# k and v of batch 2 in the row layout of q, and two vector-engine operations moved, in a fused linear-attention and SwiGLU kernel

## The chip, the cores and the metric

The kernel runs on one core of a Trainium2 chip. The metric is the device time of one execution in microseconds. Before the change the median was 326.07 us over three runs (326.01 to 326.35).

The engines are called by short names: PE is the matmul engine, PEld its weight loads, ACT the scalar engine, DVE the vector engine, POOL the GpSimd engine, SP the engine whose queue issues most of the DMAs.

## The reference

The program computes linear attention for 8 batches of 8 heads, 576 tokens and 64 columns, and puts its result through a gated feed-forward layer (512 to 1536 to 512).

```python
def phi(x, c, s):                       # c, s: cos and sin of pi/2 * pos/576
    r = np.maximum(x, 0.0)
    return np.concatenate([r * c, r * s], axis=-1)
q_p, k_p = phi(q, cos_w, sin_w), phi(k, cos_w, sin_w)
kv  = np.einsum('bhsf,bhsd->bhfd', k_p, v)      # sum over the 576 tokens
z   = np.sum(k_p, axis=2)
num = np.einsum('bhsf,bhfd->bhsd', q_p, kv)
den = np.einsum('bhsf,bhf->bhs', q_p, z)[..., None] + 1e-06
x   = (num / den).transpose(0, 2, 1, 3).reshape(4608, 512)
# ---- feed-forward
xn  = x / np.sqrt(np.mean(x * x, -1, keepdims=True) + 1e-06) * rms_g
g   = xn @ w_gate
out = (g / (1 + np.exp(-g))) * (xn @ w_val) @ w_out
```

## The kernel before

The feed-forward layer runs in nine blocks of 512 tokens: blocks 0 to 7 are the first 512 tokens of each batch, block 8 gathers the last 64 tokens of all eight. A block has 12 steps (two products of 4 wide matmuls, a Silu on ACT, a product on DVE) and 4 output steps. The attention of the next batch is hung between those steps: `at(block, step, place, function, ...)` puts a call there.

There are two layouts for k and v. The **dense** layout treats the 8 heads of a batch as one long run, 4 pairs of heads each spread over 128 partitions; a partition holds 9 tokens of one head, and one head fills 64 partitions:

```python
def load_kv(which, b, r0=0, r1=4, j0=0, j1=NJ):      # NJ = 9; one DMA
    ... in_=src[b, 2*r0:2*r1].rearrange("h s d -> (h s d)")
             .rearrange("(r p n) -> p r n", p=P, n=NJ * D)
def k_phi(eng, b, j, part, rs=(0, 4)):               # one scaling per token slot j: 9 of 256 columns
    ...
def kvz_mm(b, banks, rs=(0, 4)):
    for r in range(*rs):
        for j in range(NJ):
            for c in range(2):
                lo = 64 * c                          # 64 rows: half of the array
                nc.tensor.matmul(banks[c][:, r*E:(r+1)*E],
                    lhsT=kp_main[b][lo:lo+64, j, r, :], rhs=vvm[b % 2][lo:lo+64, r, j, :],
                    start=(j == 0), stop=(j == NJ - 1))      # 4 * 9 * 2 = 72 matmuls
```

The layout **of q** gives every head all 128 partitions with 4 tokens each, and treats the last 64 tokens of each head apart, in a tail:

```python
def load_heads(which, b, h0, h1):                    # tokens 0..511 of some heads, rows of 4 tokens
    ...
def load_last(which, b):                             # tokens 512..575: two DMAs of 64 KB
    ...
def k_phi_as_q(eng, b, c, part):                     # 4 scalings of 512 columns, one of 256
    ...
def v_cast_as_q(eng, b, h0, h1):                     # two casts on DVE
    ...
def v_cast_last(eng, b):                             # two small casts of the tail, on POOL
    ...
def kvz_as_q(b, pst):
    for h in range(H):
        for c in range(5):                           # 8 * 5 = 40 matmuls of 128 rows
            nc.tensor.matmul(pst[:, h % 2, h//2*E:(h//2+1)*E], lhsT=kp_of(b)[...],
                rhs=vv_of(b)[:, c, h, :] if c < 4 else vvt[b % 2][:, h, :], ...)
```

Batches 0 to 2 are dense in the kernel before, batches 3 to 7 have the layout of q. The turn from the outputs of block 0 to block 1 reads as follows (`tr1(j, ...)` is a PE transpose of x and an ACT copy `xnT<-psV`; `x_sq` squares and sums on ACT, with a small power on POOL; `x_norm` and `out_store(V, ...)` run on DVE):

```python
    for n in range(NNT - 2):
        ...
        if n in nd_at:                       # n = 4, 6, 8, 9
            ...
            x_sq(1, j)
        ...
    x_norm(1, 2)
    tr1(1, psV[1][:, :])
    for j in (2, 3):
        for n in (NNT - 2, NNT - 1):
            out_mm(0, j, n, banks0[j])
    out_store(V, 0, 2, banks0[2])
    out_store(A, 0, 3, banks0[3])
    for j in (0, 1):
        for n in (NNT - 2, NNT - 1):
            out_mm(0, j, n, banks0[j])
    gval_mm(1, 0, 0, (0, 256))               # first matmuls of block 1
    ...
```

The program ends with the last output tile in two halves, each copied by ACT and stored by two DMAs, one from SP and one from ACT.

Of the kernel before, what the change touches and what calls it, by code (L numbers as in the profile page):

```python
# [26 lines left out]
def kernel(  # L27
# [30 lines left out]
    psA = ps.tile([P, 2, 512], FP32, name="psA")  # L58
# [8 lines left out]
    V, A, G = nc.vector, nc.scalar, nc.gpsimd  # L67
    NJ = 9
    LOW, HIGH = (0, 2), (2, 4)
# [4 lines left out]
    def load_kv(which, b, r0=0, r1=4, j0=0, j1=NJ):  # L74

        key = (which, b)
        if key not in raw:
            raw[key] = (two if which == "k" else one).tile(
                [P, 4, NJ * D], FP32, name=f"r{which}", tag=f"r{which}"
            )  # L80
        src = {"k": k, "v": v}[which]
        return nc.sync.dma_start(
            out=raw[key][:, r0:r1, j0 * D : j1 * D],
            in_=src[b, 2 * r0 : 2 * r1, :, :]
            .rearrange("h s d -> (h s d)")
            .rearrange("(r p n) -> p r n", p=P, n=NJ * D)[:, :, j0 * D : j1 * D],
        )
# [31 lines left out]
    def load_heads(which, b, h0, h1):  # L119
        src = {"k": k, "v": v}[which]  # L120
        nc.sync.dma_start(
            out=kv_tile(which, b)[:, h0 * 4 * D : h1 * 4 * D].rearrange(
                "p (h n) -> p h n", n=4 * D
            ),
            in_=src[b, h0:h1, 0:512, :].rearrange("h (p j) d -> p h (j d)", j=4),
        )
# [131 lines left out]
    def k_phi(eng, b, j, part, rs=(0, 4)):  # L258

        o = slice(0, D) if part == 0 else slice(D, F)  # L260
        f = cos_of if part == 0 else sin_of
        if b not in kp_main:
            kp_main[b] = one.tile([P, NJ, 4, F], BF16, name="kpm", tag="kpm")
        phi(
            eng, kp_main[b][:, j, rs[0] : rs[1], o],
            raw[("k", b)][:, rs[0] : rs[1], j * D : (j + 1) * D], f(5 + j),
        )
# [237 lines left out]
    def x_norm(b, j):  # L505
        xn = four.tile([P, DM], BF16, name="xn", tag="xn")
        nc.vector.scalar_tensor_tensor(  # L507
            out=xn[:, :], in0=x_of[(b, j)][:, 0:DM], scalar=rs_of[(b, j)][:, :], in1=gb[:, :],
            op0=ALU.mult, op1=ALU.mult,
        )  # L510
        xn_of[(b, j)] = xn
# [22 lines left out]
    def x_tr_evac(eng, b, j, bank, part=(0, 4)):  # L534
        dst = bank.bitcast(BF16).rearrange("p (t s) -> p t s", s=P)
        copy(eng, x_dst(b, j)[:, part[0] : part[1], :], dst[:, part[0] : part[1], :])
# [5 lines left out]
    def gval_mm(blk, n, bank, cols=(0, TB), parts=((psG, wg), (psV, wv))):  # L542
        x = xnT[blk]
        for pst, w in parts:
            for t in range(NDT):
                nc.tensor.matmul(  # L546
                    pst[bank][:, cols[0] : cols[1]],
                    lhsT=w[:, t, n * P : (n + 1) * P],
                    rhs=x[:, t, cols[0] : cols[1]],
                    start=(t == 0), stop=(t == NDT - 1),  # L550
                )
# [19 lines left out]
    def out_store(eng, blk, j, bank):  # L571
        osb = four.tile([P, DM], FP32, name="osb", tag="osb")
        copy(eng, osb[:, :], bank)
        rows0 = out[0:S, :].rearrange("(p j) m -> j p m", j=NJ)
        if blk == 0:
            for i in range(2):
                nc.sync.dma_start(
                    out=rows0[2 * j + i, :, :], in_=osb[64 * i : 64 * i + 64, :]
                )
        elif blk < 8:  # L580
            rows = out[blk * S : blk * S + 512, :].rearrange("(p j) m -> p j m", j=4)
            nc.sync.dma_start(out=rows[:, j, :], in_=osb[:, :])
        else:
            for i in range(2):
                r0 = (2 * j + i) * S + 512
                nc.sync.dma_start(
                    out=rows0[8, :, :] if i + j == 0 else out[r0 : r0 + 64, :],
                    in_=osb[64 * i : 64 * i + 64, :],
                )
# [181 lines left out]
    def at(blk, n, where, f, *args):  # L771
        slots.setdefault((blk, n), none())[where].append((f, args))
# [26 lines left out]
    for nb in range(2, B):  # L799
        b = nb - 1  # L800
        late = nb == 2
        vb, vn = (b, 3) if late else (b - 1, 14)
        if nb == 3:
            vb, vn = b, 1
        if late:
            at(vb, vn, "post", v_cast, V, nb, *LOW)
            for j in range(NJ):
                if j > 3:
                    at(b, 1 + j // 7, "post", k_phi, V, nb, j, 0)
                if j > 1:  # L810
                    at(b, 1 + j // 7, "post", k_phi, A, nb, j, 1)
        else:
            for c in range(5):
                at(b - 1, 12 + (c * 3) // 5, "post", k_phi_as_q, V, nb, c, 0)
                at(b - 1, 12 + (c * 3) // 5, "post", k_phi_as_q, A, nb, c, 1)
        for c in range(5):
            qn = (2, 3, 5, 5, 6)[c] if late else c
            at(b, qn, "post", q_phi, V, nb, c, 0)
            at(b, qn, "post", q_phi, A, nb, c, 1)
            at(b, qn, "post", q_tr_dma, nb, c)  # L820
        if late:
            at(vb, vn + 1, "post", v_cast, V, nb, *HIGH)
        else:
            at(vb, vn, "post", v_cast_as_q, V, nb, 0, 4)
            at(vb, vn + 1, "post", v_cast_as_q, V, nb, 4, 8)
            at(vb, vn, "post", v_cast_last, G, nb)
        kz, nds = (6, (7, 9, 11, 12)) if late else (4, (5, 7, 9, 11))
        at(b, kz, "pe", kvz_pe if late else kvz_as_q, nb, psA)
        at(b, kz, "pre", kvz_evac, A, nb, psA, 0)
        at(b, kz, "pre", kvz_evac, A, nb, psA, 1)  # L830
        for j in range(4):
            n = nds[j]
            at(b, n, "mid" if n == NNT else "pe", nd_pe, nb, j, psA)
            at(b, n, "pre", nd_post, nb, j, psA)
            at(b, n, "post", x_sq, nb, j)
            where = "pre" if n + 1 >= NNT else "post"
            at(b, n + 1, where, x_norm, nb, j)
            at(b, n + 1, where, x_tr_dma, nb, j)
        if nb % 2 == 1:
            at(b, 13, "pe", nd_pe, nb, 4, psA)  # L840
            at(b, 13, "pre", nd_post, nb, 4, psA)
            at(b, 13, "post", x_sq, nb, 4)
            at(b, 14, "post", x_norm, nb, 4)
            at(b, 14, "post", x_tr_dma, nb, 4)
    for nb in range(3, B):

        b = nb - 2
# [42 lines left out]
    for n in range(NNT - 2):  # L890
        if n == 3:
            kvz_pe(1, psA)
            kvz_evac(A, 1, psA, 0)
            kvz_evac(V, 1, psA, 1)
        if 1 <= n <= 4:
            c = n - 1
            q_tr_pe(1, c, qbank[c])
            q_tr_evac(V if c < 2 else A, 1, c, qbank[c])
        if n == 0:
            for c in (1, 2, 3):  # L900
                q_phi(V, 1, c, 0)
                q_phi(A, 1, c, 1)
        if n == 1:
            v_cast(A, 1, *LOW)
            v_cast(V, 1, *HIGH)
        if n == 3:
            d = load_q_tail(1)
            tc.add_manual_dep(d.ins, wo_dmas[1].ins.name, SYNC_DEP, reason="after wo")
            load_kv("k", 2)
            load_q(2)  # L910
            load_q_tail(2)
            load_kv("v", 2)
        if n == 7:
            x_norm(1, 0)
        if n == 9:
            x_norm(1, 1)
            tr1(0, psV[0][:, :])
        for j in range(2) if n == 9 else ():
            out_mm(0, j, n, banks0[j])
        if n in nd_at:  # L920
            j = nd_at[n]
            nd_pe(1, j, psA)
            nd_post(1, j, psA)
            x_sq(1, j)
        for j in range(2 if n == 9 else 0, 4):
            out_mm(0, j, n, banks0[j])
    x_norm(1, 2)
    tr1(1, psV[1][:, :])
    for j in (2, 3):
        for n in (NNT - 2, NNT - 1):  # L930
            out_mm(0, j, n, banks0[j])
    out_store(V, 0, 2, banks0[2])
    out_store(A, 0, 3, banks0[3])
    for j in (0, 1):
        for n in (NNT - 2, NNT - 1):
# [2 lines left out]
    out_store(A, 0, 1, banks0[1])  # L938
    tr1(2, psA[:, 0, :])
    x_norm(1, 3)  # L940
    out_store(V, 0, 0, banks0[0])
    gval_mm(1, 1, 1, (0, 256), ((psG, wg),))
    x_tr_pe(1, 3, psC[1][:, :])
    x_tr_evac(V, 1, 3, psC[1][:, :])
    gval_mm(1, 1, 1, (0, 256), ((psV, wv),))
    for j in range(4):
        k_phi(V, 2, j, 0)
    for j in range(2):
        k_phi(A, 2, j, 1)
    for n in range(2):  # L950
        gval_mm(1, n, n, (256, 512))
        gval_h(1, n, n, gval_act(1, n, n))
# [64 lines left out]
```

## Time and profile before

| | before |
|---|---|
| device time, median | 326.07 us |
| profiled execution (a run of its own), device time and span | 325.86 and 324.1 us |
| PE, DVE, ACT, POOL busy | 98, 57, 54, 12% |
| chain that ends last | 90% PE, 5% DVE, 2% ACT |
| kv product of batch 2, wide group before it to second wide group after it | 65.52 to 68.87 |
| idle of PE at the turn to block 1 | 54.90 to 55.21 |

A busy time is how long an engine has instructions in it; PE's matmuls overlap, so the printed length of a group is longer than what it costs, and one reads start to start. A group of four wide matmuls costs 0.863 us that way. With PE at 98%, a saving elsewhere counts only where PE waits.

### The profile page before, as it was taken

How to read it: one execution, taken by the hardware profiler on the slowest of the kernel's cores; microseconds unless marked ns; L12 is line 12 of the kernel's file. 1: busy time of each engine (PE TensorE's matmuls, PEld its weight loads, DVE VectorE, ACT ScalarE, POOL GpSimd, SP SyncE). 2: the span in 40 equal slices, each digit the busy share in tenths (PEclk: the TensorE clock that was granted, in tenths of full speed). 3: DMA queues.
4: the chain of work that ended last, by engine and by line, in shares of the span. 5: the costliest groups of instructions: out<-in, count | busy, mean ns of one | idle time of the engine just before them, and what ended most of it. 6: DMA issues, size and time to landing. Idle time of an engine off the chain costs nothing.

```text
span 324.1 us, 6166 instructions
## 1 busy us (share of the span) xinstructions
PE 317.8 (98%) x2284; PEld 162.2 (50%) x2284; DVE 184.7 (57%) x398; ACT 173.9 (54%) x351; POOL 39.1 (12%) x85
## 2 busy tenths in 40 slices
PE   8999999999999999999999999999999999999995
PEld 2587465555445444544454445444544444444443
DVE  6975768777666765577257745772577133203410
ACT  6974865964665466545555466455644333223321
POOL 4660202001110120012001120120011000000000
PEclk9999999999999999999999999999999999999999
DMA  7999999798899676977598769766611400020014
GB/s 272 286 200 253 307 238 345 197 172 203 164 244 265 182 208 160 240 152 203 162 215 201 156 219 211 191 163 216 127 38 33 131 32 0 27 105 0 1 32 100
DMA packets 89377, 53.90 MB, mean 166 GB/s; under 512 B 56321, under 2 KB 81921, under 8 KB 89346
## 3 DMA queue, kind: packets, MB, share of 16 engines
q1 hardware_dynamic: 82304, 48.65, 58.1%
q0 software_dynamic: 6880, 4.72, 9.9%
q8 instruction: 18, 0.29, 0.4%
q10 hardware_dynamic: 162, 0.13, 0.2%
q14 instruction: 13, 0.11, 0.1%
HBM read 37.75 MB, written 9.44 MB: 146 GB/s over the span
## 4 chain that ended last, share of the span: by engine, by line
PE 90%; DVE 5%; ACT 2%; DMA 1%; issue 1%; DVEq 0%; ACTq 0%
PE psG L546 26%; PE psC L566 26%; PE psV L546 26%; PE psA L414 2%; PE psA L370 2%; DVE kpm L254 1%; PE psG L693 1%; PE psV L693 1%; DMA rk<-in_k_dram 1%; PE psO L693 1%; PE psG L566 1%; DVE vvm L339 1%; ACT kpm L252 1%; DVE qp L254 1%; PE psA L386 1%
## 5 line engine op out<-in xcount | busy, mean ns | idle before, releaser
L561 DVE TENSOR_TENSOR hT<-psV,sg 128x512 bf16<-128x512 f32 x102 | 70.3, 689 | 95.9 <-PE psV L546 85.5
L555 ACT ACTIVATE sg<-psG 128x512 f32<-128x512 f32 x102 | 60.7, 595 | 64.8 <-PE psG L546 64.7
L546 PE MATMUL psG<-xnT,wg 128*128 128x512 bf16 (+1 forms) x368 | 92.8, 374 | 0.3 <-DVE xnT L339 0.2
L546 PE MATMUL psV<-xnT,wv 128*128 128x512 bf16 (+1 forms) x368 | 92.7, 374 | 0.0
L566 PE MATMUL psC<-wo,hT 128*128 128x512 bf16 x396 | 89.4, 379 | 0.0
L546 PEld LDWEIGHTS <-wv 128*128 128x128 bf16 x416 | 40.7, 98 | 47.3
L566 PEld LDWEIGHTS <-hT 128*128 128x128 bf16 x420 | 40.1, 98 | 46.5
L546 PEld LDWEIGHTS <-wg 128*128 128x128 bf16 x416 | 38.5, 98 | 41.2 <-DVE osb L339 0.6
L485 POOL TENSOR_TENSOR rs<-ms,mhalf 128x1 f32<-128x1 f32 x36 | 19.8, 551 | 188.7 <-ACT scr L480 188.7
L337 ACT COPY osb<-psC 128x512 f32<-128x512 f32 (+1 forms) x33 | 19.1, 579 | 43.1 <-PE psC L566 42.3
L507 DVE SCALAR_TENSOR_TENSOR xn<-xt,rs,gb 128x512 bf16<-128x512 f32 x35 | 26.5, 758 | 16.6 <-POOL rs L485 16.5
L480 ACT ACTIVATE scr<-xt 128x513 bf16<-128x513 f32 x36 | 22.8, 635 | 23.9 <-DVE xt L469 23.8
L252 ACT ACTIVATE kpm<-rk,tab 128x256 bf16<-128x256 f32 (+2 forms) x58 | 28.2, 545 | 1.5 <-DMA rk<-in_k_dram 1.5
L469 DVE TENSOR_TENSOR xt<-psA,rec 128x512 f32<-128x512 f32 x35 | 24.2, 691 | 1.2
L252 ACT ACTIVATE qp<-rq,tab 128x512 bf16<-128x512 f32 (+1 forms) x37 | 23.7, 662 | 0.0
L254 DVE TENSOR_SCALAR kpm<-rk,tab 128x128 bf16<-128x128 f32 (+2 forms) x64 | 20.3, 375 | 2.1 <-DMA rk<-in_k_dram 2.1
L254 DVE TENSOR_SCALAR qp<-rq,tab 128x512 bf16<-128x512 f32 (+1 forms) x37 | 16.1, 454 | 0.0
L414 PEld LDWEIGHTS <-qpT 128*128 128x128 bf16 x248 | 11.6, 98 | 6.8 <-ACT qpT L337 0.2
L414 PE MATMUL psA<-kvzs,qpT 128*128 128x65 bf16 x248 | 12.8, 194 | 0.1
L546 PE MATMUL psG<-xnt_tail,wg 128*128 128x512 bf16 x48 | 12.3, 379 | 0.0
L546 PE MATMUL psV<-xnt_tail,wv 128*128 128x512 bf16 x48 | 12.3, 379 | 0.0
L339 DVE CAST vvm<-rv 128x1024 bf16<-128x1024 f32 (+4 forms) x16 | 10.7, 694 | 0.0
(99 smaller groups left out, 183.0 us busy)
## 6 DMA issues: line engine op xcount, KB each, us to landing
out_dram<-osb SPq DMA_DIRECT2D x28, 256.0 KB, 2.5
rk<-in_k_dram SPq DMA_DIRECT2D x20, 256.0 KB, 3.3
rq<-in_q_dram SPq DMA_DIRECT2D x20, 256.0 KB, 3.1
rv<-in_v_dram SPq DMA_DIRECT2D x16, 256.0 KB, 3.2
rq<-in_q_dram SPq DMA_DIRECT2D x2, 1024.0 KB, 8.7
out_dram<-osb SPq DMA_DIRECT2D x14, 128.0 KB, 3.2
rv<-in_v_dram SPq DMA_DIRECT2D x3, 576.0 KB, 7.9
wo<-in_moe_w_out_dram POOLq DMA_DIRECT2D x4, 384.0 KB, 7.2
```

What stands on the lines that cost most here:

```text
L252: nc.scalar.activation(out=out_ap, in_=in_ap, func=AF.Relu, scale=scale)
L254: eng.tensor_scalar(out=out_ap, in0=in_ap, scalar1=scale, scalar2=0.0, op0=ALU.mult, op1=ALU.max)
L337: nc.scalar.copy(out=o, in_=i)
L414: nc.tensor.matmul(o[:, g, i, :], lhsT=qpT[(b, 0)][:, h, j * P : (j + 1) * P], rhs=kvz_of(b, h), start=True, stop=True,)
L469: nc.vector.tensor_tensor(out=xt[:, 0:DM].rearrange("p (b h d) -> p b h d", b=2, d=D), in0=o[:, :, :, 0:D], in1=rec[:, :, :].unsqueeze(3). ...
L480: nc.scalar.activation(out=scr[:, :], in_=xt[:, 0 : DM + 1], func=AF.Square, scale=1.0 / math.sqrt(DM), accum_out=ms[:, :],)
L485: nc.gpsimd.tensor_tensor(out=rs[:, :], in0=ms[:, :], in1=mhalf[:, :], op=ALU.pow)
L507: nc.vector.scalar_tensor_tensor(out=xn[:, :], in0=x_of[(b, j)][:, 0:DM], scalar=rs_of[(b, j)][:, :], in1=gb[:, :], op0=ALU.mult, op1=ALU. ...
L546: nc.tensor.matmul(pst[bank][:, cols[0] : cols[1]], lhsT=w[:, t, n * P : (n + 1) * P], rhs=x[:, t, cols[0] : cols[1]], start=(t == 0), sto ...
L555: nc.scalar.activation(out=sg[:, :], in_=psG[bank][:, :], func=AF.Silu)
L561: nc.vector.tensor_tensor(out=hTs[blk][:, n, :], in0=psV[bank][:, :], in1=sg[:, :], op=ALU.mult)
L566: nc.tensor.matmul(bank, lhsT=hTs[blk][:, n, j * P : (j + 1) * P], rhs=wo[:, n, :], start=(n == 0), stop=(n == NNT - 1),)
```

## The change

The intent: PE does the kv product of batch 2 with 40 matmuls on all rows instead of 72 on half of them, ACT and DVE have fewer and larger scalings, and two orders on DVE are changed so that PE's next operands or banks come sooner.

```diff
@@ schedule of batch nb; late is nb == 2 @@
         if late:
-            at(vb, vn, "post", v_cast, V, nb, *LOW)
-            for j in range(NJ):
-                if j > 3:
-                    at(b, 1 + j // 7, "post", k_phi, V, nb, j, 0)
-                if j > 1:
-                    at(b, 1 + j // 7, "post", k_phi, A, nb, j, 1)
+            for c in range(1, 5):
+                if c > 1:
+                    at(b, 1 + c // 4, "post", k_phi_as_q, V, nb, c, 0)
+                at(b, 1 + c // 4, "post", k_phi_as_q, A, nb, c, 1)
...
-        if late:
-            at(vb, vn + 1, "post", v_cast, V, nb, *HIGH)
-        else:
-            at(vb, vn, "post", v_cast_as_q, V, nb, 0, 4)
-            ...
+        at(vb, vn, "post", v_cast_as_q, V, nb, 0, 4)
+        at(vb, vn + 1, "post", v_cast_as_q, V, nb, 4, 8)
+        at(vb, vn, "post", v_cast_last, G, nb)
...
-        at(b, kz, "pe", kvz_pe if late else kvz_as_q, nb, psA)
+        at(b, kz, "pe", kvz_as_q, nb, psA)
@@ loads @@
-            load_kv("k", 2)
+            load_heads("k", 2, 0, 8)
+            load_last("k", 2)
             load_q(2)
             load_q_tail(2)
-            load_kv("v", 2)
+            load_heads("v", 2, 0, 8)
+            load_last("v", 2)
@@ turn @@
-    x_norm(1, 2)
     tr1(1, psV[1][:, :])
...
     out_store(V, 0, 2, banks0[2])
+    x_norm(1, 2)
     out_store(A, 0, 3, banks0[3])
...
     x_norm(1, 3)
-    out_store(V, 0, 0, banks0[0])
     gval_mm(1, 1, 1, (0, 256), ((psG, wg),))
     x_tr_pe(1, 3, psC[1][:, :])
     x_tr_evac(V, 1, 3, psC[1][:, :])
+    out_store(V, 0, 0, banks0[0])
...
-    for j in range(4):
-        k_phi(V, 2, j, 0)
-    for j in range(2):
-        k_phi(A, 2, j, 1)
+    for c in range(2):
+        k_phi_as_q(V, 2, c, 0)
+    k_phi_as_q(A, 2, 0, 1)
```

More of the change, by code (lines that the diff above doesn't have):

```diff
@@ L820 @@
             at(b, qn, "post", q_tr_dma, nb, c)
-        if late:
-            at(vb, vn + 1, "post", v_cast, V, nb, *HIGH)
-        else:
-            at(vb, vn, "post", v_cast_as_q, V, nb, 0, 4)
-            at(vb, vn + 1, "post", v_cast_as_q, V, nb, 4, 8)
-            at(vb, vn, "post", v_cast_last, G, nb)
+        at(vb, vn, "post", v_cast_as_q, V, nb, 0, 4)
+        at(vb, vn + 1, "post", v_cast_as_q, V, nb, 4, 8)
+        at(vb, vn, "post", v_cast_last, G, nb)
         kz, nds = (6, (7, 9, 11, 12)) if late else (4, (5, 7, 9, 11))
-        at(b, kz, "pe", kvz_pe if late else kvz_as_q, nb, psA)
+        at(b, kz, "pe", kvz_as_q, nb, psA)
         at(b, kz, "pre", kvz_evac, A, nb, psA, 0)
```

## The prediction

> **What bounds the kernel now.** I read the page's first part and its chain first, then the timeline of the matmul engine around the two places that the diff touches, then short windows inside the slow group.
>
> ```profile
> PE 317.8 (98%) x2284; PEld 162.2 (50%) x2284; DVE 184.7 (57%) x398; ACT 173.9 (54%) x351; POOL 39.1 (12%) x85
> ...
> PE 90%; DVE 5%; ACT 2%; DMA 1%; issue 1%; DVEq 0%; ACTq 0%
> ```
>
> The matmul engine (PE) is occupied nearly all the time, and 90% of the chain that ends last is matmuls. From 68 to 320 us the PE timeline has no idle to speak of. So the change is worth only what it takes off PE's own row before 68 us: matmul issue time removed, or PE gaps closed. Work removed from DVE or ACT (57% and 54% busy) counts only where PE waits for it.
>
> The kv product of batch 2, and the same product of batch 3, which already has the layout that the change brings to batch 2 (columns: start us, us, engine, line, operation, shapes, count):
>
> ```profile
> 65.52 1.03 PE L546 MATMUL psV<-xnT,wv 128*128 128x512 bf16 x4
> 66.48 1.58 PE L386 MATMUL psA<-vvm,kpm 64*128 64x65 bf16 x72
> 67.99 1.04 PE L546 MATMUL psG<-xnT,wg 128*128 128x512 bf16 x4
> 68.87 0.38 PE L546 MATMUL psV<-xnT,wv 128*128 128x512 bf16 x1
> ```
>
> ```profile
> 96.23 1.03 PE L546 MATMUL psV<-xnT,wv 128*128 128x512 bf16 x4
> ...
> 98.31 1.02 PE L546 MATMUL psG<-xnT,wg 128*128 128x512 bf16 x4
> 99.17 1.03 PE L546 MATMUL psV<-xnT,wv 128*128 128x512 bf16 x4
> ```
>
> Look at the starts, since the printed lengths overlap. A group of 4 wide matmuls takes 0.863 us from start to start. Batch 2: from 65.52 to 68.87 is 3.35 us; less two such groups (1.73) the kv product costs 1.62. Batch 3: from 96.23 to 99.17 is 2.94, less 1.73 is 1.21. Where the 1.62 goes (columns: PE busy with count, weight loads with count, clock, DMA share, GB/s, for the kv matmuls alone):
>
> ```profile
> 67.00:67.10 0.10, 0.10 (x16) 0.10 (x9) 1.00 0.94 72
> 67.10:67.20 0.10, 0.10 (x9) 0.03 (x2) 1.00 0.28 102
> 67.20:67.30 0.10, 0.03 (x2) 0.00 (x0) 1.00 0.56 174
> 67.30:67.40 0.10, 0.10 (x7) 0.09 (x7) 1.00 0.69 236
> ```
>
> Weight loads stop at about 67.1 and resume at 67.3: the second half of the heads waits for the second cast of v, which on DVE is this line, ending at 67.25:
>
> ```profile
> 66.50 0.75 DVE L339 CAST vvm<-rv 128x1152 bf16<-128x1152 f32 x1
> ```
>
> So 1.62 is about 1.26 of issue (batch 1 ran the same 72 matmuls in 1.26 us, 43.54 to 44.80), 0.25 of that wait and 0.1 before the group. Second place, the turn from block 0's output to block 1:
>
> ```profile
> 54.04 1.03 PE L566 MATMUL psC<-wo,hT 128*128 128x512 bf16 x4
> 54.43 0.68 DVE L339 COPY osb<-psG 128x512 f32<-128x512 f32 x1
> ...
> 54.60 0.57 ACT L337 COPY xnT<-psV 128x512 bf16<-128x512 bf16 x1
> ...
> 55.16 0.36 PEld L546 LDWEIGHTS <-wg 128*128 128x128 bf16 x4 [0.59 <-DVE osb L339]
> 55.21 0.60 PE L546 MATMUL psG<-xnT,wg 128*128 128x256 bf16 x4
> ...
> 56.74 0.39 PE L532 MATMUL psC<-ident,xn 128*128 128x128 bf16 x4
> ...
> 57.24 0.42 DVE L339 COPY xnT<-psC 128x512 bf16<-128x512 bf16 x1 [0.53 <-PE psC L532]
> ...
> 57.72 0.61 PE L546 MATMUL psG<-xnT,wg 128*128 128x256 bf16 x4 [0.15 <-DVE xnT L339]
> ```
>
> The output matmuls stop issuing at 54.04 + 0.86 = 54.90, the next start at 55.21: 0.31 us idle, put down to the DVE copy of the third output, which ends at 55.11. But ACT's copy of xnT ends at 55.17, and that is an operand of the same matmuls. The program's listing of waits agrees: the weight load waits for DVE, the first matmul for ACT. The second gap, 0.15 us, ends when the copy of the last x transpose does.
>
> **What the Trainium skill says.** (1) "TensorEngine Tiling (Array Packing)", Key Properties: changing the tiling mode drains the engine. The trace agrees: the 64-row group starts 0.10 us after the wide matmuls before it would let it (65.52 + 0.86 = 66.38), the batch 3 group with full rows starts at once (97.09). (2) "TensorE: Matmul & The Clock Gate", Part 1, "Wait — 56ns, not 53.3ns?": start to start is N over 2.4 GHz plus about 2.5 ns, so 29.6 ns at 65 columns; the trace has 1.22 us / 40 = 30.5 ns, near enough. (3) The same page and part, "Architectural detail": ACT and DVE take instructions strictly in order. The trace agrees: ACT's copy of xnT begins at 54.60 as ACT's square of the fourth x (from 53.97) ends, though PE's transposes for it began at 52.96. (4) "DMA: Bandwidth & Descriptors", Specifications: rows of at least 512 B are needed for line rate. No line of this trace isolates it; the new tail loads have rows of 256 B.
>
> **The change part by part.** *Layout of k and v of batch 2.* PE: 72 matmuls of 64 rows become 40 of 128 rows. 1.62 becomes 1.21, the figure of batch 3: **-0.41 us**, of which only 0.05 is issue, 0.1 the mode switch and about 0.25 the wait for the cast. The last holds only if the cast comes in time. DVE: 9 scalings of 256 columns (about 0.29 each) become 4 of 512 (0.43) and one of 256: 2.6 to 2.1 us. ACT: 9 at about 0.42 become 4 at about 0.64 and one at 0.45: 3.8 to 3.0. I followed both queues with the new order. ACT is done with its last k scaling some 0.4 us earlier, so the Silu of step 3 starts near 63.1 instead of 63.62; DVE's product behind it near 63.7 instead of 64.23; the first v cast ends near 65.4, the second near 66.6 instead of 67.25. PE starts the group at 66.38 and wants the fifth head 0.61 later, at 66.99: the wait should be gone, with 0.3 us to spare. GpSimd gets two small casts of v's tail, 0.94 us for the pair in batch 3, on an engine that is idle from 55.3 to 72.9.
>
> *Loads.* The bytes are the same, but two loads become six, with 1 KB and 256 B rows instead of 2.3 KB. Now v of batch 2 is issued and lands so:
>
> ```profile
> 48.85 0.73 SPq L82 DMA_DIRECT2D rv<-in_v_dram x1
> ```
>
> with 9.7 us to landing, so at 58.6. The DMA share is above 1 up to 55 us, so the stream is bound by the engines and pieces arrive in order of issue. My estimate for four tail loads at worse than line rate and longer issue is 1 to 3 us later: v near 60, its tail near 61.5. Needed: 64.7 for the first cast, about 65.3 for the tail. Hidden. The queue then issues block 0's stores, which wait for those landings, then q's transposes, at 64.09 now and after k pieces that take 1.1 us; there are about 1.9 us of room there. Hidden too.
>
> *The two moves.* The third output's copy gets in front of the third norm: it ends near 54.5 instead of 55.11, and releases the bank. But ACT's copy at 55.17 does not move, so PE still starts at about 55.2: **0 to -0.05 us**. The norm ends at 55.2, PE wants it at 56.0. Moving the first output's copy behind the last x copy frees nothing: it was over at 56.70, before the x copy could start (57.24, after the transposes of 56.74). It now pushes the first k scalings 0.6 us back, but the first product (59.00) waits for ACT anyway. 0.
>
> Sum: -0.41 - 0.02 = -0.43 us. After this PE is back to back, so the gain carries to the end: 326.07 - 0.43 = 325.64, say **325.6 us**.
>
> **Rivals.** (a) *A late transfer takes the place of the wait*: v's tail lands after 65 us, PE waits for GpSimd in the kv product. For it: in batch 3 GpSimd waits for just that load, and ends only 0.15 us or so before PE begins its group. Against it: the 3 us of room worked out above. Worth up to +1 us, giving 326 to 327. (b) *The gap at 54.90 is DVE's alone*, and ACT's copy is seen in time anyway: then the first move gives all 0.3, and the total is -0.7, 325.3. For it: the profile names DVE; against it: ACT's end is 0.06 us later than DVE's. (c) *The gain is eaten at batch 3's kv product*, where the casts are tight. DVE there is itself paced by PE's results (it waits for them at 92.18 and 93.91), so the casts should move forward with PE; if not, half the gain goes: 325.9.
>
> **Range and chances.** Most likely 325.4 to 325.8, from -0.7 to -0.25, with a run spread of some 0.2 (326.01 to 326.35 before). Adding the milder half of (a) gives 325.2 to 326.1. 2% is 6.5 us, fifteen times the gain: faster 0.5%, same 99%, slower 0.5%.
>
> **What would show it.** Right: 40 matmuls of 128 rows in 1.22 us with no gap before or inside; second v cast over by 66.7; next wide group some 0.4 earlier against its own start; PE's start at the turn still near 55.2 with ACT as the releaser. Wrong: PE waiting for GpSimd or DVE inside the kv product, a start at 54.9, or a q transpose landing late so that the first numerator product (69.73 now) waits.

## The result, and the profile after

| | before | after |
|---|---|---|
| device time, median of 5 runs | 326.07 us | 325.94 us |
| lowest to highest | 325.92 to 326.35 | 325.77 to 326.01 |
| profiled execution, device time | 325.86 | 325.77 |

The ratio is 0.9995, with a 95% interval of 0.9981 to 1.0008: the same. The difference of the medians, 0.13 us, is less than a third of the 0.43 that the sum of the prediction gave. What follows is a hunt for 0.3 us in 326.

The first part and the chain on the page of the kernel after: 32 matmuls fewer on PE, POOL 1.4 us busier.

```profile
PE 317.7 (98%) x2252; PEld 162.3 (50%) x2252; DVE 183.9 (57%) x394; ACT 173.2 (53%) x347; POOL 40.5 (12%) x87
...
PE 93%; ACT 3%; DVE 2%; DMA 1%; issue 1%; DVEq 0%; ACTq 0%
```

The kv product of batch 2 in the timeline after (columns: start us, us, engine, line, operation, shapes, count, then idle time and releaser if any), in the order PE, DVE, POOL:

```profile
65.60 1.03 PE L546 MATMUL psV<-xnT,wv 128*128 128x512 bf16 x4
66.46 0.28 PE L370 MATMUL psA<-vvm,kpm 128*128 128x65 bf16 x4
...
67.68 1.02 PE L546 MATMUL psG<-xnT,wg 128*128 128x512 bf16 x4
68.54 1.03 PE L546 MATMUL psV<-xnT,wv 128*128 128x512 bf16 x4
...
65.96 0.68 DVE L339 CAST vvm<-rv 128x1024 bf16<-128x1024 f32 x1
...
60.51 0.94 POOL L339 CAST vvt<-rv 64x256 bf16<-64x256 f32 x2 [4.86 <-DMA rv<-in_v_dram]
```

From 65.60 to 68.54 is 2.94 us where it was 3.35. The first kv matmul starts at 66.46 = 65.60 + 0.86, so there is no gap before the group; from 66.46 to 67.68 the 40 matmuls take 1.22 us; the second cast of v ends at 65.96 + 0.68 = 66.64. The windows view of the same stretch, for those matmuls alone (columns: window, length, PE busy with count, weight loads with count, clock, DMA share, GB/s), has no hole where the old one had weight loads stopping:

```profile
66.80:67.00 0.20, 0.20 (x13) 0.20 (x10) 1.00 0.54 108
67.00:67.20 0.20, 0.20 (x13) 0.20 (x10) 1.00 0.86 241
```

The turn in the timeline after:

```profile
54.12 1.03 PE L566 MATMUL psC<-wo,hT 128*128 128x512 bf16 x4
...
53.89 0.69 DVE L339 COPY osb<-psG 128x512 f32<-128x512 f32 x1
...
54.68 0.56 ACT L337 COPY xnT<-psV 128x512 bf16<-128x512 bf16 x1
...
54.77 0.10 PEld L546 LDWEIGHTS <-wg 128*128 128x128 bf16 x1
...
55.29 0.60 PE L546 MATMUL psG<-xnT,wg 128*128 128x256 bf16 x4
```

The DVE copy is now over at 54.58, but PE still stops issuing at 54.12 + 0.86 = 54.98 and starts again at 55.29: the same 0.31 us of idle. ACT's copy ends at 54.68 + 0.56 = 55.24. The first weight load (PEld), which waited for the DVE copy before, now runs at 54.77, half a microsecond ahead of its matmul: the DVE copy no longer holds PE, the ACT copy does.

Now follow the gain to the end. PE ran 0.08 us behind the kernel before when it came to the turn (54.12 against 54.04) and to the kv product (65.60 against 65.52); at 68.54 it was 0.33 ahead. The last copy on ACT starts 0.33 ahead as well, so nothing is lost in the 251.55 us between them. Before, in the timeline:

```profile
320.42 0.37 ACT L337 COPY osb<-psG 128x256 f32<-128x256 f32 x1 [0.94 <-PE psG L977]
```

After:

```profile
320.09 0.37 ACT L337 COPY osb<-psG 128x256 f32<-128x256 f32 x1 [0.94 <-PE psG L973]
```

And yet the device times differ by 0.09 only. From the start of that copy to the end of the device time it is 325.86 - 320.42 = 5.44 us before and 325.77 - 320.09 = 5.68 after: the kernel after loses 0.24 us **from the start of its last compute instruction on**, where the diff changes nothing. The waits of the SP queue show where to look, though not how much it costs: the kernel "four more small loads, after" below has 1.3 in this line and no loss (columns: queue, line, what it waited for: us in total, times, longest). Before:

```profile
SPq L1012 <- DMA out_dram<-osb: 1.1, 1, 1.1
```

After:

```profile
SPq L1008 <- DMA out_dram<-osb: 1.6, 2, 1.1
```

These lines are the program's last, the waits for all DMAs. The compiled program tells what they are. Every DMA issued by SP or ACT signals one of eight semaphores, which are given out in rotation, and at the end SP waits for the eight in a fixed order, one instruction each:

```
SP: wait SW semaphores; wait DMAHW0; wait DMAHW1; ... wait DMAHW7; drain; barrier
last eight DMAs, before (229 in all): SP 7, SP 0, SP 1, SP 2, ACT 3, SP 4, ACT 5, SP 6
last eight DMAs, after  (233 in all): SP 3, SP 4, SP 5, SP 6, ACT 7, SP 0, ACT 1, SP 2
```

The change adds four DMAs, so the last stores move by four places in the rotation. In both kernels the last to land is ACT's last store. Before, it sits at place 5, and once it has landed two waits (6 and 7) and the drain are left. After, it sits at place 1, near the head of the list: SP stands there until it lands, and then still has six waits to go through. That is the theory that the experiments test; 0.24 us over four places would be 0.06 us a place, an estimate (measured below).

### The profile page after: what moved, and what is told of

Read it like the earlier page. It is cut to its first block, busy times and chain, and to the rows that moved or that the text cites. A ratio compares the mean times of both kernels' runs of the same rounds, so it can differ in the third digit from the quotient of the medians.

```text
span 324.0 us, 6104 instructions
## 1 busy us (share of the span) xinstructions
PE 317.7 (98%) x2252; PEld 162.3 (50%) x2252; DVE 183.9 (57%) x394; ACT 173.2 (53%) x347; POOL 40.5 (12%) x87
## 4 chain that ended last, share of the span: by engine, by line
PE 93%; ACT 3%; DVE 2%; DMA 1%; issue 1%; DVEq 0%; ACTq 0%
PE psG L546 27%; PE psV L546 27%; PE psC L566 26%; PE psA L370 2%; PE psA L414 2%; ACT kpm L252 2%; PE psG L693 1%; DMA rk<-in_k_dram 1%; PE psV L693 1%; PE psO L693 1%; PE psG L566 1%; PE psV L321 1%; PE psA L386 1%; PE psA L422 0%; DVE xn L507 0%
## 5 line engine op out<-in xcount | busy, mean ns | idle before, releaser
L252 ACT ACTIVATE kpm<-rk,tab 128x512 bf16<-128x512 f32 (+2 forms) x54 | 27.5, 564 | 1.6 <-DMA rk<-in_k_dram 1.6
L254 DVE TENSOR_SCALAR kpm<-rk,tab 128x512 bf16<-128x512 f32 (+2 forms) x60 | 20.3, 394 | 2.1 <-DMA rk<-in_k_dram 2.1
L339 DVE CAST vvm<-rv 128x1024 bf16<-128x1024 f32 (+4 forms) x16 | 10.0, 653 | 0.0
```

What stands on the lines that cost most here:

```text
L252: nc.scalar.activation(out=out_ap, in_=in_ap, func=AF.Relu, scale=scale)
L254: eng.tensor_scalar(out=out_ap, in0=in_ap, scalar1=scale, scalar2=0.0, op0=ALU.mult, op1=ALU.max)
```

## The experiments

Each kernel ran five times, and the kernel before ran nine times beside it on the same chip: 326.03 us median for the first four experiments, 326.02 for the next four, 326.02 for the last three. "Tail" is the device time of the profiled run less the start of ACT's last copy.

### Layout alone

The new layout, with both moves undone:

```diff
+    x_norm(1, 2)
     tr1(1, psV[1][:, :])
...
     out_store(V, 0, 2, banks0[2])
-    x_norm(1, 2)
...
     x_norm(1, 3)
+    out_store(V, 0, 0, banks0[0])
...
     x_tr_evac(V, 1, 3, psC[1][:, :])
-    out_store(V, 0, 0, banks0[0])
```

> Only the layout of k and v of batch 2; the two moves undone. Theory A (the gain sits on the matmul engine and carries to the end; the rest of the difference between 0.41 and the measured 0.13 is scatter of the first loads and of the last stores): from the wide matmuls before the kv product to those behind it 2.94 us as in the changed kernel (3.35 before), and a median 0.2 to 0.5 us below the kernel before of the same rounds. Theory B (something at the end that is not tied to the matmul engine takes the gain back each time): the same 2.94, but a median within 0.15 us of before, and a longer time from the last matmul to the end of the span.

Measured: 325.88 us (325.74 to 326.12), ratio 0.9993 (0.998 to 1.0005). From wide group to second wide group 65.93 to 68.88, so 2.95; tail 326.12 - 320.43 = 5.69. The profiled run is the slowest of the five. What the change does to the time, on PE and at the end, is all found in the layout.

### The two moves alone

The moves, with the old layout: the part "turn" of the diff without its last seven lines.

```diff
-    x_norm(1, 2)
     tr1(1, psV[1][:, :])
...
     out_store(V, 0, 2, banks0[2])
+    x_norm(1, 2)
...
-    out_store(V, 0, 0, banks0[0])
...
     x_tr_evac(V, 1, 3, psC[1][:, :])
+    out_store(V, 0, 0, banks0[0])
```

> Only the two moves of x norm and output copies; the layout as before. If ACT's copy of xnT gates the turn as much as DVE's copy of the output does: the idle stretch of 0.31 us ahead of block 1's first matmuls stays at 0.28 to 0.32 us, total within 0.15 us of before. If DVE alone was the gate: idle stretch gone, total 0.3 us less.

Measured: 326.09 us (325.97 to 326.23), ratio 0.9999 (0.9987 to 1.0012). The timeline at the turn:

```profile
54.26 1.03 PE L566 MATMUL psC<-wo,hT 128*128 128x512 bf16 x4
...
54.81 0.56 ACT L337 COPY xnT<-psV 128x512 bf16<-128x512 bf16 x1
...
55.43 0.60 PE L546 MATMUL psG<-xnT,wg 128*128 128x256 bf16 x4
```

From 54.26 to 55.43 is 1.17, less 0.86 of issue: 0.31 us idle, as before. The DVE copy had been over since 54.72, so DVE was not what PE waited for; ACT's copy ended at 55.37. The tail is 5.44, as before: no DMA was added.

### ACT's copy early, DVE's late

The kernel before, with ACT's square of the fourth x put behind its copy of `xnT`:

```diff
         if n in nd_at:
             ...
-            x_sq(1, j)
+            if j < 3:
+                x_sq(1, j)
...
     tr1(1, psV[1][:, :])
+    x_sq(1, 3)
```

> The kernel before with one thing changed: ACT copies the second x transpose of batch 1 out of PSUM ahead of its square of the fourth x, not behind it. ACT's copy should end near 54.1 instead of 55.17. If both engines gate the turn, DVE's copy of the output (55.11) still holds it: start within 0.06 us of before, total within 0.15 us. If ACT alone was the gate, 0.3 us less.

Measured: 325.95 us (325.89 to 326.13), ratio 0.9996 (0.9983 to 1.0008). The timeline (the first line is two ACT copies run together):

```profile
53.05 1.13 ACT L337 COPY xnT<-psV 128x512 bf16<-128x512 bf16 x2
...
54.65 0.68 DVE L339 COPY osb<-psG 128x512 f32<-128x512 f32 x1
...
55.39 0.61 PE L546 MATMUL psG<-xnT,wg 128*128 128x256 bf16 x4
```

ACT is done at 54.18, and PE still starts at 55.39, right after DVE's copy ends at 55.33. The gap went from 0.31 to 0.27. Each of the two copies alone holds PE.

### Both gates

The kernel after, with the same four lines, so that both copies that PE waits for (the two gates) are done early:

```diff
-            x_sq(1, j)
+            if j < 3:
+                x_sq(1, j)
...
     tr1(1, psV[1][:, :])
+    x_sq(1, 3)
```

> The changed kernel with the same reordering on ACT: both gates released early. If the turn waits for the later of the two, the idle stretch of 0.31 us is closed and the total is 0.3 us below the changed kernel, some 0.7 us below before (theory A), with a risk that the fourth x norm, which ends near 56.43, now is what the matmul engine waits for. Theory B: total as the changed kernel although the matmul engine ends 0.3 us earlier.

Measured: 325.53 us median, but in two groups: 325.48, 325.52, 325.53 and 326.33, 326.52; ratio 0.9987 (0.9974 to 1.0001). The timeline of the profiled execution, which is the slowest of the five:

```profile
54.27 1.03 PE L566 MATMUL psC<-wo,hT 128*128 128x512 bf16 x4
...
55.13 0.60 PE L546 MATMUL psG<-xnT,wg 128*128 128x256 bf16 x4
...
100.38 0.42 PE L414 MATMUL psA<-kvzs,qpT 128*128 128x65 bf16 x8 [0.65 <-DMA qpT<-qp]
```

The gap is gone: 54.27 + 0.86 = 55.13. So the two waits are an AND, and the first move is worth nothing alone and 0.31 us together with an order on ACT that the change does not have. In this execution PE then waited 0.65 us at 100.38 for the first transpose of q of batch 3 by DMA. It took 6.5 us from issue to landing, where the same transpose took 4.4 in the kernel before and 5.0 in the kernel after; and it was issued 0.76 us later than in the kernel after (93.85 against 93.09). The tail is 326.52 - 320.77 = 5.75, with the same DMA numbering as the kernel after.

### Four more small loads, after

Four loads of 256 bytes each, early in block 7, that read into a row no longer used. They do nothing but shift the rotation by four, back to where the kernel before has it.

```diff
+    def spare_load(i):
+        nc.sync.dma_start(out=g_row[:, 64*i:64*i+64],
+            in_=moe_rms_g.rearrange("(o d) -> o d", o=1)[:, 64*i:64*i+64])
...
+    for i in range(4):
+        at(7, 4, "post", spare_load, i)
```

> The changed kernel with four loads of 256 bytes more, late in block 7 where the SP queue is idle; they rewrite a row that nobody reads any more. They shift by four places on which of the eight DMA semaphores the last stores land. Theory B in its new form (SP waits for the eight in a fixed order at the end, and in the changed kernel the last store's is the third of them, in the kernel before the seventh; each wait left behind the last landing costs some 60 ns): from the start of ACT's last copy to the device time 5.44 us as in the kernel before, not 5.7 as in the changed one, and a median 0.2 to 0.3 us below the changed kernel, near 325.65. Theory A (scatter): no change beyond 0.1 us.

Measured: 325.67 us (325.63 to 325.82), ratio 0.9991 (0.9979 to 1.0004): 0.35 us below the kernel before of the same rounds, and 0.27 below the kernel after of its own rounds. The timeline:

```profile
320.24 0.37 ACT L344 COPY osb<-psG 128x256 f32<-128x256 f32 x1 [0.94 <-PE psG L982]
```

The profiled run took 325.66, so the tail is 5.42. A kernel with more DMAs ends sooner.

### Four more small loads, before

The same lines in the kernel before.

> The same four loads added to the kernel before, whose last stores then land on the semaphores that they have in the changed kernel. Theory B: 5.7 us from ACT's last copy to the device time instead of 5.44, median 0.2 to 0.3 us above before, near 326.3. Theory A: within 0.1 us of before.

Measured: 326.33 us (326.30 to 326.45), ratio 1.0011 (0.9998 to 1.0023), 0.31 slower than the kernel before, and not one of its five runs is as fast as the slowest of that one's nine (326.28). The timeline:

```profile
320.61 0.37 ACT L344 COPY osb<-psG 128x256 f32<-128x256 f32 x1 [0.94 <-PE psG L986]
```

With 326.31 of the profiled run the tail is 5.70. The same four loads shorten the tail of one kernel and lengthen that of the other by as much. It is not their number that counts but where the last stores come to lie among the eight.

### The second cast of v early

The kernel before, with the second cast of v one step earlier, to measure the wait in the old kv product:

```diff
         if late:
-            at(vb, vn + 1, "post", v_cast, V, nb, *HIGH)
+            at(vb, vn, "post", v_cast, V, nb, *HIGH)
```

> The kernel before with the second cast of v of batch 2 one step earlier on DVE; no DMA and no matmul changed. If 0.25 of the 0.41 us was the wait for that cast: the 72 matmuls take 1.26 us from start to the next group instead of 1.51, and with the DMA count unchanged the whole 0.25 shows in the total, near 325.8. If the 1.51 is the issue of 72 matmuls: no change.

Measured: 325.86 us (325.72 to 325.92), ratio 0.9995 (0.9983 to 1.0008). The timeline:

```profile
66.56 1.34 PE L386 MATMUL psA<-vvm,kpm 64*128 64x65 bf16 x72
67.83 1.04 PE L546 MATMUL psG<-xnT,wg 128*128 128x512 bf16 x4
```

The 72 matmuls take 1.27 us from their start to the next group, where the kernel before takes 67.99 - 66.48 = 1.51. So 0.24 us of the predicted gain were the wait for the cast, and moving that cast one step earlier in the schedule removes it without any new layout. Tail 5.45.

### Fewer loads elsewhere

The kernel of "both gates", with k of batch 3 in two loads of four heads instead of four of two, and its v in one load instead of two, to bring the number of DMAs down to 230 and the last store to place 7:

```diff
+            if (which, nb) == ("k", 3):
+                at(b, 0, "post", load_heads, "k", nb, 0, 4)
+                at(b, 2, "post", load_heads, "k", nb, 4, 8)
+                at(b, 4, "post", load_last, "k", nb)
+                continue
...
-                at(b, 13, "post", load_heads, "v", nb, 0, 4)
-                at(b, 14, "post", load_heads, "v", nb, 4, 8)
+                at(b, 14, "post", load_heads, "v", nb, 0, 8)
```

> The changed kernel with the two gates of e4 open and three loads fewer (k of batch 3 in two loads of four heads, v of batch 3 in one), so that the last store's semaphore is the last of the eight, and the SP queue has less to issue before the transposes of q of batch 3, for which e4 waited 0.65 us in its slow executions. Theory B: 0.7 us off the matmul engine and a tail no longer than before's: near 325.25, and fewer or no executions near 326.4. Theory A: as e4's fast executions, 325.5. If one load of 1 MB for v holds up others, the wait for the transpose stays.

Measured: 326.12 us (325.73 to 327.19), ratio 1.0 (0.9986 to 1.0014), a miss. The tail was 327.19 - 321.75 = 5.44, as it should be, but PE now waits for v of batch 3 (timeline):

```profile
97.44 0.28 PE L370 MATMUL psA<-vvm,kpm 128*128 128x65 bf16 x4 [0.57 <-DVE vvm L339]
...
99.03 0.28 PE L370 MATMUL psA<-vvm,kpm 128*128 128x65 bf16 x4 [0.70 <-DVE vvm L339]
```

The first cast waited for the one load (issued at 88.83) until 96.69, where with two loads in "both gates" (the first issued at 88.61) it began at 94.43. This is the slowest of the five executions, and the loads of k were changed too, so how much of the miss is v's in the others is not shown. Adding loads that carry nothing was the better way to shift the rotation.

### Both gates and four small loads

"Both gates" with the four loads of 256 bytes; the diff is that of these two experiments together.

> The changed kernel with both gates of the turn open (as e4) and the four late small loads (as e5), so that the last stores land on the semaphores of the kernel before. Matmul engine 0.72 us ahead of before, tail 5.44: 325.3 in its fast executions. The wait for the transpose of q of batch 3 that e4 showed should stay in some executions, at 326.1 or so, since nothing before block 7 differs from e4.

Measured: 325.35 us (325.24 to 325.59), ratio 0.9976 (0.9963 to 0.9989); tail 325.30 - 319.88 = 5.42. No execution was slow.

### The same, with a transpose later

To give the SP queue room before q's transposes of batch 3, the transpose of the last x of batch 1 is issued in block 2:

```diff
-    at(1, 15, "post", x_tr_dma, 1, 4)
+    at(2, 3, "post", x_tr_dma, 1, 4)
```

> As e9, with one DMA moved: the transpose of the fifth x piece of batch 1, which nobody needs before the last block, is issued three steps of block 2 later, behind the transposes of q of batch 3 instead of ahead of them. If the SP queue's order is what made that transpose late, no execution is slow: all within 0.2 us of 325.3. If the DMA engines themselves are full there, the slow executions stay.

Measured: 325.33 us (325.26 to 325.38), ratio 0.9975 (0.9962 to 0.9987), tail 5.44. The timeline has the turn closed, 54.26 + 0.86 = 55.12:

```profile
54.26 1.03 PE L573 MATMUL psC<-wo,hT 128*128 128x512 bf16 x4
...
55.13 0.60 PE L553 MATMUL psG<-xnT,wg 128*128 128x256 bf16 x4
```

This is the fastest of all kernels tried. The move of the transpose itself is not shown to do anything: the kernel without it had no slow execution either in five. Why "both gates" alone had two slow ones in five stays open. Up to block 7 it is the same program as "both gates and four small loads", so two slow ones in five against none may be chance; what differed in the profiled one was when the SP queue got to its work.

### All but the layout

The kernel before with the two moves, the order on ACT and the early cast:

```diff
-            x_sq(1, j)
+            if j < 3:
+                x_sq(1, j)
...
     tr1(1, psV[1][:, :])
+    x_sq(1, 3)
...
-            at(vb, vn + 1, "post", v_cast, V, nb, *HIGH)
+            at(vb, vn, "post", v_cast, V, nb, *HIGH)
```

> The kernel before, k and v of batch 2 in the old layout, with the two moves, the ACT order of e3 and the early cast of e7. No DMA added. Matmul engine 0.31 + 0.25 = 0.56 us ahead of before, tail 5.44: 325.45. If that holds, the new layout itself is worth only the remaining 0.15 us on the matmul engine, less than its four loads cost at the end (0.24).

Measured: 325.58 us (325.52 to 326.03), ratio 0.9985 (0.9972 to 0.9999). The turn costs 0.86, the kv matmuls run from 66.50 to 67.77, so 1.27, and the tail is 325.66 - 320.20 = 5.46. This is 0.25 us above the best kernel of the same rounds. In the profiled runs 0.12 of that is the start of the program (ACT's first scaling begins at 4.68 against 4.56). So the layout, once the cast is in time, is worth some 0.15 us on PE by the rows (0.05 of issue, and the 0.10 before the group that the prediction puts down to the mode switch), and it gives back 0.24 at the end unless the rotation is put right.

## Why the prediction was right or wrong

The predicted 325.6 lies 0.34 below the measured 325.94. That is outside the 325.4 to 325.8 called most likely, and inside the wider 325.2 to 326.1 by luck: the range was widened for rival (a), a late transfer, which did not come, and another cost took its place. "The same" was safe, since 2% is 6.5 us. The terms of the sum, against the profiled pair:

| term | predicted | measured | from |
|---|---|---|---|
| kv product of batch 2 | -0.41 | -0.41 | 65.52 to 68.87 (3.35) became 65.60 to 68.54 (2.94) |
| first move | 0 to -0.05 | 0.00 | idle of 0.31 both times |
| second move | 0 | 0.00 | PE keeps its distance of 0.08 to the kernel before, 57.80 against 57.72 |
| start of the program | not in the sum | +0.08 | PE at 54.12 against 54.04 |
| after the last copy | not in the sum | +0.24 | 5.68 against 5.44 |
| sum | -0.43 | -0.09 | 325.77 - 325.86 |

**The kv product: right in size and in mechanism.** 0.41 was read off batch 3 and came out. Its parts hold too: 0.24 of wait in the experiment that moves the cast (predicted "about 0.25"), no gap before the group, and the second cast over at 66.64 (predicted 66.6). The chain behind it was followed rightly: the Silu of step 3 started at 63.14 (63.1 predicted), the product behind it at 63.75 (63.7).

**The turn: right, and the rival (b) refuted.** Taking DVE's copy out of the way left 0.31 (moves alone), taking ACT's out left 0.27, and taking both left nothing. The profile's releaser, DVE, was one of two; in the program's listing the weight load waits for DVE and the matmul behind it for ACT, and the trace after agrees (weight load at 54.77, matmul at 55.29). The prediction's check, that ACT's end is 0.06 us later than DVE's, was what told it.

**The loads: right that they are hidden from PE, wrong that this ends their account.** v was issued at 52.07 and its tails at 52.65 instead of 48.85, and POOL could cast the tail at 60.51, near the "61.5" of the estimate and far ahead of the 65.3 needed. Rival (a) did not show in the profiled run. Nor did (c): PE ran without a wait through the kv product of batch 3 in the kernel after.

**The step that failed** is "After this PE is back to back, so the gain carries to the end". It carries to ACT's last copy, to the hundredth. But the sum left out a term, the end of the program, which the four added loads change: 0.24 us, more than half of the gain. The prediction counted six loads instead of two and asked only when they land. The two experiments with four empty loads show the term with both signs (5.70 in the kernel before, 5.42 in the kernel after), and all thirteen profiled kernels fall into two groups by the place of their last stores: 5.42 to 5.46 us with the last store at place 6 or 7, 5.68 to 5.75 with it at place 2. The packed traces also hold SP's waits one by one, which no view prints, and they show where the time goes:

| us | before | after | fewer loads |
|---|---|---|---|
| place of the last store to land | 5 | 1 | 6 |
| from the start of ACT's last copy to the end of SP's wait for that store | 2.62 | 2.61 | 2.68 |
| from there to SP's drain | 0.21 (2 waits) | 0.46 (6 waits) | 0.13 (1 wait) |
| from the drain to the end of the device time | 2.60 | 2.60 | 2.62 |

In the four kernels with place 1 SP needs 0.46 us for the six waits and to get to its drain, in the eight with place 5 it needs 0.19 to 0.22 for two. After the first, each wait follows the one before it by 0.06 us, though all these semaphores are already set. So four more waits make the 0.24. In "fewer loads" the place is better by one more, and a landing 0.06 later hides it. Places other than 1, 5 and 6 were not tried.

The remaining 0.08 us, before the turn, is scatter of the first loads: the kernels reach the turn at 54.04 to 54.46. ACT's first scaling of k, which waits for the first load, starts at 4.43 in the kernel after and at 4.34 in the kernel before, and in twelve of the thirteen profiled runs PE reaches the turn 49.68 to 49.70 us after it. The thirteenth is the layout alone (50.12), where PE also waits 0.27 us for a weight at 17.97.

## What to carry to other kernels

When an engine waits for the results of two others, as PE did for a copy on DVE and one on ACT, look at when each of them ends before you move one: the profile names one, and here only both together gave the 0.31 us. A gain of tenths of a microsecond must be followed to the end of the device time, since adding DMAs anywhere may shift which of a set of reused semaphores the last stores signal; here that alone was worth 0.24 us, and it can be measured by adding loads that do nothing. Before you rebuild a layout to shorten a group of matmuls, ask how much of the group is a wait: here 0.24 of 0.41 us were one cast issued a step too late.

## What the Trainium skill lacked or had wrong

- The end of a program has a cost that depends on which semaphores the last stores use: 5.42 to 5.46 us from the last copy's start to the end of the device time against 5.68 to 5.75, by four places in a rotation of eight. The Trainium skill, "Runtime: NRT & Kernel Launch", section "The ~15µs preamble/postamble breakdown", has three entries for the end (a barrier of about 1.5 us, the reset of semaphores, and a barrier with the reset of the DMA rings), and nothing that the program's own waits for its DMAs would add, 0.06 us each here; the page "DMA: Bandwidth & Descriptors" has nothing of it either.
- "TensorEngine Tiling (Array Packing)", Key Properties, says that a change of the tiling mode drains the engine, without a number: the 64-row group of batch 2 started 0.10 us late here (66.48 against 66.38), and the full-row group that replaces it did not (66.46 = 65.60 + 0.86).
- "SBUF — State Buffer", section "🎯 Summary: rules for kernel authors", says that when DVE has two SBUF inputs and the GpSimd instruction reads SBUF, the second one to issue is fully blocked until the first finishes. In the kernel after, POOL's small power starts at 54.85 beside DVE's norm (54.50 to 55.24, two inputs in SBUF) and takes 0.80 us instead of 0.55. It is 0.80 in all eight kernels with the first move and 0.55 in all five without it. It got 0.25 longer, which is less than the 0.39 for which the norm still ran: the direction agrees; a block for the whole overlap is not shown by this pair, and times on POOL are rough.
